# An mLSTM with two expert layers on one core: first gate chunk broadcast by masked matmuls, second gate round issued later, plain transposes, low bits on ScalarE

## The chip, the cores and the metric

One Trainium2 chip; the kernel runs on one core of it. The metric is the device time of one execution in microseconds (us): the median of three runs. Engines are named as in the profile: PE is TensorE (PEld its weight loads), DVE is VectorE, ACT is ScalarE, POOL is GpSimd, SP is SyncE, which issues every DMA of this kernel.

## What is computed

Three layers follow one another. The first is an mLSTM over 2 batches, 8 heads, 768 positions and head size 40, written in the reference as a recurrence:

```python
m_new = np.maximum(f_gate[:, :, t] + m, i_gate[:, :, t])
f_stab = np.exp(f_gate[:, :, t] + m - m_new)
i_stab = np.exp(i_gate[:, :, t] - m_new)
C = f_stab * C + i_stab * einsum('bhd,bhe->bhde', vt, kt)
n = f_stab * n + i_stab * kt
h_tilde = einsum('bhde,bhe->bhd', C, qt)
denom = np.maximum(np.abs(sum(n * qt)), 1.0)
y = sigmoid(o_gate) * h_tilde / denom
```

Its output, 1536 tokens of 320 features, goes through a layer of 2048 hidden units with a rational activation, P(h)/(Q(h) + 1e-6) with a cubic P and Q = 1 + |b0||h| + |b1|h^2 (weights w_in and w_out), and then through four ReLU experts of 1024 hidden units, whose outputs are summed with normalised probabilities.

## The kernel before

The mLSTM is worked in chunks of 128 positions: 6 chunks by 2 batches give 12 steps (`attn_steps`, i = 0 to 11, even i for batch 0). A step makes a decay matrix per head by a scan on DVE (`s_w`, L410) from forget gates that PE has broadcast over 128 partitions, multiplies it into q·k scores (`s_sc` L440, `s_pm` L445), multiplies by v scaled with the input gate (`s_v` L430, `s_pv` L470), adds the state carried from earlier chunks (`s_inter` L464), renews that state (`s_kend` L456 or L454, `s_delta` L485 to L490) and divides and gates the result (`s_y`, L498 to L505). `s_x` turns the 128 x 320 result into feature-major halves: `to_xT` transposes it on PE and splits it into a rounded part and a remainder (L526, L527). The features fill two blocks of 128 and one of 64. The last 64 are wanted twice, on both halves of the partitions: with DX=1 that is done by two full transposes (L521), one of 64 columns (L523) and one fp32 matmul into partitions 64 to 127 (L524, two passes in the trace).

The gates come in two rounds. `gates1` makes e = exp(...) for chunk 0 of all 16 rows (batch times head) in a tile of 48 partitions: forget gates in rows 0 to 15, input gates in rows 32 to 47. `gates1_bc(b)` broadcasts the forget gates of a batch's 8 heads with 8 fp32 matmuls (L302; 16 PE passes in the trace), and `gates1_ist` transposes the input gates. `gates2` does the other five chunks at once: a scan (L314), `gate_x` (five subtractions and additions on POOL, GX='G'), `exps` (two sigmoids on ACT, a reciprocal and a product on DVE), a scan (L321) and two calls of `expand`, which split the result into high and low parts and spread it with `mask` into the tiles fm and cm (L326 to L332). Step 2 is the first that reads fm (`bcast_f`, L344).

The first layer's weights come as 64-bit floats, seen as pairs of 32-bit integers. 22 pieces of 128 x 512 (`win_piece`, `wout_piece`) are loaded into two staging buffers (tag stg, SB=2) and converted by `conv64`: ACT takes the high word's magnitude (L187), POOL copies the high word (L199) and writes the top bits of the low word over it (L196; on ACT, L193, for one piece), DVE joins them (L201); then ACT rounds to fp32r (L159) and DVE or POOL subtracts for the remainder (L168). A staging buffer is free again after L187, L199 and L196 or L193 have read it.

The first layer runs in 48 units (`mono_unit`), each 16 matmuls of 128 x 256 (L544), an activation over ACT, DVE and POOL (`e_mono`) and 12 matmuls into an accumulator (L571 to L573). The experts follow: expert 0 in 24 units woven between the last mono units, then experts 1 to 3.

The order of the work is set by a table of times, KP. Every step, unit, piece and gate round is an event with a due time; events are emitted in that order (`emit`), which is the order of priority for the program's scheduler, and that fixes each engine's queue ahead of the run. GS, GD, SO, SO2, T1, PS, PP, MS, MP and TP are such times; letter strings such as L3, GLE, LO, SU, ve, ke, eh0 and el1 name the engine for each piece, unit or step. P0 is the number of pieces emitted ahead of everything but step 0's loads and gates.

Of the kernel before, what the change touches and what calls it, by code (L numbers as in the profile page):

```python
# [8 lines left out]
F32 = mybir.dt.float32  # L9
F32R = mybir.dt.float32r  # L10
AF = mybir.ActivationFunctionType
ALU = mybir.AluOpType
# [8 lines left out]
def kernel(  # L21
# [17 lines left out]
    P = 128  # L39
    B, NC, _, D = qk.shape[:4]  # L40
    H = kv.shape[4]
    S = NC * P
    DM = H * D
    NT = B * NC
    BH = B * H
# [9 lines left out]
    KP = dict(  # L55
        UP='PPPPPPPPPPPPPPPPPPPPPPPPPPPPPPPPPPPPPPPPPPPPPPPP',
        SU='GGGGGGGGGGGGGGGGGGGGGGGGGGGGGGVVVVVVVVGGGGGGGGGG',
        GLE='GGGGGGVGGGGGGGGGGGGGGGGGGGGGGGGGGGGGGGGVVGVGGGGG', L3='GGGGGGGGGGGGGGGGGGAGGG', P0=1, GS=2.5, GD=9.21,
        SO=1.69, SO2=13.47, T1=4.63, GX='G', KB=0, DA='VVVVVVVAAAAA', DX=1, ce='PPPPPPPPPPPP', CD=1, TG='SXX',
        TB=(2, 2, 2), HB=2, APR=0, APS=0, CPR=0, XPR=0, FPR=0, LPR=0, EPR=0, SG='GGGGGGGGGGGGGGGGGGGGGG',  # L60
        LO='VVGVVGVVGVVGVVGVVGVVGV', QC=1, qce='VGVVVVVVVVVV', cde='GGGGGGGGGGGG', ve='GGGGGGGGAGGG',
        ke='AGGGGGGGGGGA', xe='VVVVVVVVVVVV', XB=3, YB=4, RB=2, GB=2, FB=2, SB=2, VR=1, V1=2, XT=2, CB=2, LAGA=4,
        LAGB=4, TP=10.02, SP=1.13, MS=20.29, MP=5.0, PS=4.6, PP=1.11, LEAD=5, XR=0.69, XE=3, E0S=-6.11, E0P=2.33,
        E1S=1.27, eh0='AAGGAA', el0='VGVVVV', eh1='GAGGGG', el1='VGGGGG', qv=1.2, CVP='SSSSSSSSSSSSSSSSSSSSSS', EX='V', dv=-0.86, X2=1)
    YB, FB = KP["YB"], KP["FB"]

    V, A, G, PE, SY = nc.vector, nc.scalar, nc.gpsimd, nc.tensor, nc.sync

    ENG = dict(A=A, G=G, V=V)
# [37 lines left out]
    ident = cp.tile([P, P], F32, name="ident")  # L107
# [9 lines left out]
    sel = at1.tile([P, 2, 4], F32R, name="sel")  # L117
# [4 lines left out]
    mask = at1.tile([P, 4], F32, name="mask")  # L122
# [23 lines left out]
    def load_o(c):  # L146
        SY.dma_start(out=so[:, 2 * c:2 * c + 2, :], in_=o_gate[:, 2 * c:2 * c + 2, :])
# [17 lines left out]
    def split_lo(eng, dst, src, hi):  # L165
        k = n_conv[0] - 1
        eng = eng or (V if KP["CVP"][k] == "P" else ENG[KP["LO"][k]])
        eng.tensor_tensor(out=dst, in0=src, in1=hi.bitcast(F32), op=ALU.subtract)  # L168
# [91 lines left out]
    S0 = P + NA * P  # L260
    NX = NA * P
    n0 = 2 * S
    x1_, s11, s21, e1_ = [ga[0:48, n0 + n * P:n0 + (n + 1) * P] for n in range(4)]
    m_, gtmp = gb[0:BH, 0:S + 1], gb[0:BH, S + 1:2 * S + 1 - P]
    n0 = 2 * S + 4 - P
    d1, x2_, s12, s22 = [gb[0:112, n0 + n * NX:n0 + (n + 1) * NX] for n in range(4)]
    e2_, cd = [gc_[0:112, n * NX:(n + 1) * NX] for n in range(2)]
    fm, cm = [at1.tile([P, NA, 4, P], F32R, name=n) for n in ("fm", "cm")]
    ist = cp.tile([P, NC, BH], F32, name="ist")
    V.memset(m_[:, 0:1], -1e30)  # L270
    V.memset(x1_, 0.0)
# [10 lines left out]
    def gate_x(eng, a, z, outs):  # L282
        tmp = gtmp[:, 0:z - a]
        eng.tensor_tensor(out=tmp, in0=fr[:, a:z], in1=m_[:, a:z], op=ALU.add)
        for x, r, u, w in outs:
            eng.tensor_tensor(out=x[r:r + BH, 0:w - u], in0=tmp[:, u - a:w - a], in1=m_[:, u + 1:w + 1], op=ALU.subtract)
            eng.tensor_tensor(out=x[r + 32:r + 32 + BH, 0:w - u], in0=ir[:, u:w], in1=m_[:, u + 1:w + 1],
                              op=ALU.subtract)

    g1_last = []  # L290

    def gates1():
        V.tensor_tensor_scan(m_[:, 1:P + 1], fr[:, 0:P], ir[:, 0:P], -1e30, op0=ALU.add, op1=ALU.max)
        gate_x(V, 0, P, [(x1_, 0, 0, P)])
        exps(e1_, x1_, s11, s21)
        g1_last.append(V.memset(e1_[0:BH, 0:1], 0.0))

    def gates1_bc(b):
        bc = [(pa_p, f"acc{j}") if b == 0 else (ph_p, "h") for j in range(2)]
        bc = [p_.tile([P, U], F32, tag=t_, name=f"bc{b}") for p_, t_ in bc]  # L300
        for h in range(H):
            PE.matmul(bc[h // 4][:, (h % 4) * P:(h % 4 + 1) * P],  # L302
                      ident[0:BH, b * H + h:b * H + h + 1].to_broadcast([BH, P]), e1_[0:BH, :],
                      start=True, stop=True)
        bc_t[b] = bc

    def gates1_ist():
# [2 lines left out]
        V.tensor_copy(ist[:, 0, :], tp[:, 32:48])  # L310

    def gates2():
        with tc.issue_after(g1_last[0].ins):
            V.tensor_tensor_scan(m_[:, P + 1:S + 1], fr[:, P:S], ir[:, P:S], m_[:, P:P + 1], op0=ALU.add,  # L314
                                 op1=ALU.max)
        gate_x(ENG[KP["GX"]], P, S, [(x2_, 0, P, S0), (x2_, 64, S0, S)])
        exps(e2_, x2_, s12, s22)
        for r, a, z in ((0, P, S0), (64, S0, S)):
            V.tensor_copy(d1[r:r + BH, 0:z - a:P], e2_[r:r + BH, 0:z - a:P])
            V.memset(e2_[r:r + BH, 0:z - a:P], 0.0)  # L320
        V.tensor_tensor_scan(cd, e2_, d1, 0.0, op0=ALU.mult, op1=ALU.add)  # L321
        expand(cm, cd, s12.bitcast(F32R))
        expand(fm, e2_, s22.bitcast(F32R))
# [35 lines left out]
    def small_consts(last_sig):  # L359
        V.memset(cq, 1.0 + 1e-6)  # L360
        ab1 = cp.tile([P, 1], F32, name="ab1")
        rb1 = cp.tile([P, 1], F32, name="rb1")
        ab = cp.tile([P, 1], F32, name="ab")
        SY.dma_start(out=a_t, in_=dram_ap(moe_a, 0, [[0, P], [1, 4]]))
        SY.dma_start(out=b_t, in_=dram_ap(moe_b, 0, [[0, P], [1, 2]]))
        SY.dma_start(out=pr, in_=probs)
        A.activation(ab, b_t[:, 1:2], AF.Abs)
        V.tensor_scalar(ab1, ab, 1e-30, None, op0=ALU.max)
        with tc.issue_after(last_sig.ins):
            A.activation(rb1, ab1, AF.Abs_reciprocal_sqrt)  # L370
        V.tensor_tensor(out=sb1, in0=ab1, in1=rb1, op=ALU.mult)
        V.reciprocal(rb1, sb1)
        V.tensor_tensor(out=rb1, in0=rb1, in1=ab, op=ALU.mult)
        V.tensor_tensor(out=sb1, in0=sb1, in1=rb1, op=ALU.add)
        V.tensor_scalar(sb1, sb1, 0.5, None, op0=ALU.mult)
        psum_ = cp.tile([P, NT], F32, name="psum_")
        V.tensor_reduce(out=psum_, in_=pr, axis=AX.X, op=ALU.add)
        V.tensor_scalar(psum_, psum_, 1e-9, None, op0=ALU.add)
        V.reciprocal(psum_, psum_)
        V.tensor_tensor(out=pr, in0=pr, in1=psum_.unsqueeze(2).to_broadcast([P, NT, NE]), op=ALU.mult)  # L380
# [4 lines left out]
    def attn_steps(i):  # L385
        c, b = divmod(i, B)
# [3 lines left out]
        st = {}  # L390
# [51 lines left out]

        def s_pm(j):
            pm = st["W"][:, 4 * j:4 * j + 4, :]
            V.tensor_tensor(out=pm, in0=st["sc"][j], in1=pm, op=ALU.mult)  # L445

        def s_kend():
            if c < NC - 1:
# [47 lines left out]
        def s_y():  # L496
            o, den = st["o"], st["den"]
            V.reciprocal(den, den)  # L498
            so3 = so[:, i, :].rearrange("p (h d) -> p h d", h=H)
            if KP["xe"][i] == "V":  # L500
                G.tensor_tensor(out=so3, in0=so3, in1=den.to_broadcast([P, H, D]), op=ALU.mult)
            x = st["x"] = at2.tile([P, 384], F32, tag="x", bufs=KP["XT"], name=f"x{i}")
            x3 = x[:, 0:DM].rearrange("p (h d) -> p h d", h=H)
            if KP["xe"][i] == "V":
                V.tensor_tensor(out=x3, in0=o[:, :, 0:D], in1=so3, op=ALU.mult)  # L505
            else:
                for h in range(H):
                    A.activation(x3[:, h], o[:, h, 0:D], AF.Copy, scale=den[:, h])
                G.tensor_tensor(out=x3, in0=x3, in1=so3, op=ALU.mult)
            if not KP["DX"]:  # L510
                A.activation(x[:, DM:384], x[:, 2 * P:DM], AF.Copy)
# [68 lines left out]
    def e_mono(hp):  # L580
# [20 lines left out]
        A.activation(gh, s, AF.Copy)  # L601
        ENG[KP["GLE"][k]].tensor_tensor(out=gl, in0=s, in1=gh.bitcast(F32), op=ALU.subtract)  # L602
        return gh, gl
# [62 lines left out]
    ev = []  # L666
    steps = {i: attn_steps(i) for i in range(NT)}
    TP, SP = KP["TP"], KP["SP"]
    gates1()
    load_qkv(0)  # L670
    gates1_bc(0)
    gates1_ist()
    run(pieces, KP["P0"])
# [4 lines left out]
    ev.append((KP["GS"] + KP["GD"], gates2_ist))  # L678
    ev.append((KP["SO"], lambda: sig_o(0)))
    for c in range(1, NC):  # L680
        ev.append((KP["GS"] + 0.1, lambda c=c: load_o(c)))

    def sigs():
        for c in range(1, NC):
            ls = sig_o(c)
        small_consts(ls)
    ev.append((KP["SO2"], sigs))
    mu = [(g, j) for g in range(NG) for j in range(NUA)]
    t_end = [0.0] * NT
# [8 lines left out]
    t = KP["PS"]  # L698
# [3 lines left out]
    t = KP["MS"]  # L702
    na = 0
    while True:
        g, j = mu[na]
        t = max(t, t_end[2 * g + 1] + 0.2)
# [43 lines left out]
    x_acc = {}  # L750
    LAG[0] = KP["LAGB"]

# [16 lines left out]
    ev = []  # L769
# [3 lines left out]
    t = 0.0  # L773
# [24 lines left out]
    def e1_load():  # L798
        we[1] = expert_tile(1)
        for n, f in enumerate(expert_pieces(1, we[1], KP["eh1"], KP["el1"])):  # L800
            pri(KP["EPR"], f)
    ev.append((t_m + KP["E1S"], e1_load))
    emit(ev)
# [62 lines left out]
```

## Time and profile before

| | us |
|---|---|
| median of 3 runs | 694.28 (692.99 to 696.75) |
| the profiled execution | 695.96 |
| its span, first to last instruction | 693.9 |
| PE busy in the span | 645.6 (93%) |
| DVE busy | 376.5 (54%) |
| ACT busy | 309.3 (45%) |
| POOL busy | 262.8 (38%) |

The span and the busy times belong to the one profiled execution, 1.68 us above the median. A busy time is the sum over an engine's instructions; matmuls are pipelined, so the mean duration of one is longer than the distance from one to the next. Mean values over the whole span hide that the stages have different limits.

### The profile page before, as it was taken

What the parts mean: (1) busy time and instruction counts of PE and PEld (TensorE: products, weight loads), DVE (VectorE), ACT (ScalarE), POOL (GpSimd) and SP (SyncE); (2) the same over time, 40 slices, a digit from 0 to 9 for tenths busy, and PEclk for the clock granted to TensorE, in tenths of its full rate; (3) what the DMA queues carried; (4) which work ended last, traced back from release to release, by engine and by line L of the source; (5) the groups of instructions that cost most, each with busy time, mean ns of one, the idle gap of its engine ahead of it and who ended that gap; (6) DMA issues with size and microseconds to landing.
All of it is one profiled execution on the core that took longest, in us unless ns stands there. A gap on an engine that the chain in (4) does not pass through costs nothing.

```text
span 693.9 us, 10545 instructions
## 1 busy us (share of the span) xinstructions
PE 645.6 (93%) x4202; PEld 602.6 (87%) x4202; DVE 376.5 (54%) x602; ACT 309.3 (45%) x550; POOL 262.8 (38%) x255
## 2 busy tenths in 40 slices
PE   5467599999999799999999999999999999999997
PEld 5346489999999789999999999999999999999996
DVE  7887788786887877776576422222322222213132
ACT  5563666675667797676677422211111111111111
POOL 8687876454545653222223887730000000000000
PEclk9757699999999899999999999999999999999999
DMA  8756531111101400000000344300000000001011
GB/s 257 207 171 193 165 106 57 39 39 39 39 1 31 136 3 1 1 1 1 1 1 1 84 120 132 86 21 1 1 1 0 1 1 1 0 1 39 1 38 39
DMA packets 15697, 35.67 MB, mean 51 GB/s; under 512 B 2048, under 2 KB 7424, under 8 KB 15648
## 3 DMA queue, kind: packets, MB, share of 16 engines
q1 hardware_dynamic: 15648, 35.00, 17.0%
q8 instruction: 33, 0.54, 0.3%
q14 instruction: 16, 0.13, 0.1%
HBM read 33.03 MB, written 1.97 MB: 50 GB/s over the span
## 4 chain that ended last, share of the span: by engine, by line
PE 81%; DMA 6%; POOL 5%; DVE 4%; issue 1%; ACT 1%; SPq 1%; DVEq 0%; ACTq 0%; POOLq 0%
PE h L544 37%; PE acc L573 12%; PE acc L571 12%; PE acc L572 12%; DMA stg_a<-in_moe_w_in_dram 3%; PE o L470 2%; PE sc L440 2%; POOL cv_l L196 2%; DMA stg_b<-in_moe_w_out_dram 1%; POOL cv_l L199 1%; PE o L464 1%; PE tx L524 1%; DMA qkt<-in_qk_dram 1%; PE dl L485 1%; PE tx L521 1%
## 5 line engine op out<-in xcount | busy, mean ns | idle before, releaser
L544 PE MATMUL h<-x,we 128*128 128x512 f32 (+1 forms) x960 | 194.9, 349 | 0.0
L608 DVE SCALAR_TENSOR_TENSOR gl<-h,gh 128x512 fp32r<-128x512 f32 x96 | 66.3, 691 | 218.3 <-ACT gh L607 217.9
L544 PEld LDWEIGHTS h<-x,we 128*128 128x128 f32 x960 | 154.6, 189 | 19.2 <-issue 0.5
L607 ACT ACTIVATE gh<-h 128x512 fp32r<-128x512 f32 x96 | 57.3, 598 | 239.3 <-PE h L544 148.3
L572 PE MATMUL acc<-we,gh 128*128 128x320 f32 x384 | 117.0, 309 | 0.0
L571 PE MATMUL acc<-we,gh 128*128 128x320 f32 x384 | 116.8, 309 | 0.0
L544 PE MATMUL h<-x,win 128*128 128x256 f32 x768 | 106.0, 293 | 5.7 <-DVE s__2213 L598 4.7
L544 PEld LDWEIGHTS h<-x,win 128*128 128x128 f32 x768 | 100.5, 200 | 7.5 <-issue 5.3
L573 PE MATMUL acc<-we,gl 128*128 128x320 f32 x384 | 101.7, 310 | 0.0
L571 PEld LDWEIGHTS acc<-we,gh 128*128 128x128 f32 x384 | 72.2, 188 | 2.9 <-issue 0.3
L572 PEld LDWEIGHTS acc<-we,gh 128*128 128x128 f32 x384 | 72.2, 188 | 2.6
L573 PEld LDWEIGHTS acc<-we,gl 128*128 128x128 f32 x384 | 67.9, 188 | 0.1
L571 PE MATMUL acc<-wout,gh 128*128 128x320 f32 x192 | 60.5, 318 | 0.1
L572 PE MATMUL acc<-wout,gh 128*128 128x320 f32 x192 | 59.5, 312 | 0.0
L573 PE MATMUL acc<-wout,gl 128*128 128x320 f32 x192 | 56.4, 318 | 0.8 <-POOL gl L602 0.8
L440 PE MATMUL sc<-qkt 128*128 128x128 f32 x192 | 32.4, 328 | 6.1 <-DVE fb L410 5.5
L571 PEld LDWEIGHTS acc<-wout,gh 128*128 128x128 f32 x192 | 36.9, 192 | 0.7 <-ACT gh L601 0.4
L573 PEld LDWEIGHTS acc<-wout,gl 128*128 128x128 f32 x192 | 35.4, 190 | 2.1 <-POOL gl L602 1.6
L572 PEld LDWEIGHTS acc<-wout,gh 128*128 128x128 f32 x192 | 36.8, 192 | 0.3 <-issue 0.2
L440 PEld LDWEIGHTS sc<-qkt 128*128 128x128 f32 x192 | 29.9, 237 | 8.1 <-DVE fb L410 6.5
L201 DVE SCALAR_TENSOR_TENSOR cv_t<-cv_t,cv_l 128x512 int32<-128x512 int32 x22 | 18.8, 854 | 11.1 <-POOL cv_l L196 11.0
L410 DVE TENSOR_TENSOR_SCAN fb<-bf,id 128x512 f32<-128x512 f32 x20 | 23.7, 1209 | 1.0 <-PE bf L344 1.0
(759 smaller groups left out, 1012.9 us busy)
## 6 DMA issues: line engine op xcount, KB each, us to landing
stg_b<-in_moe_w_out_dram SPq DMA_DIRECT2D x10, 512.0 KB
stg_a<-in_moe_w_in_dram SPq DMA_DIRECT2D x8, 512.0 KB
stg_c<-in_moe_w_dram SPq DMA_DIRECT2D x8, 512.0 KB
kv<-in_kv_dram SPq DMA_DIRECT2D x12, 320.0 KB
qkt<-in_qk_dram SPq DMA_DIRECT2D x24, 160.0 KB
stg_d<-in_moe_w_dram SPq DMA_DIRECT2D x8, 480.0 KB
stg_a<-in_moe_w_in_dram SPq DMA_DIRECT2D x8, 256.0 KB
stg_c<-in_moe_w_dram SPq DMA_DIRECT2D x8, 256.0 KB
```

Of the source, the lines that this page charges most:

```text
L196: G.tensor_scalar(o, i_, 0.9375 / 32, 0.0, op0=ALU.mult, op1=ALU.add)
L199: G.tensor_scalar(l3.bitcast(F32), hw.bitcast(F32), 0.0, 1.0, op0=ALU.mult, op1=ALU.mult)
L201: V.scalar_tensor_tensor(out=ti, in0=ti, scalar=3, in1=l3, op0=ALU.logical_shift_left, op1=ALU.bitwise_or)
L410: V.tensor_tensor_scan(W, src, id4f, 0.0, op0=ALU.mult, op1=ALU.add)
L440: PE.matmul(sc[j][:, p, :], qkt[b][:, p, 2 * j], qT[:, p], start=True, stop=True)
L470: PE.matmul(o[:, h, :], st["W"][:, h, :], v1[:, h, :], start=(c == 0 and h == 0), stop=(h == H - 1))
L544: PE.matmul(o, w5[:, j, fs], r, start=(n == 0), stop=(n == len(seq) - 1))
L571: PE.matmul(acc[t], lh, wh, start=(first and a == 0), stop=False)
L572: PE.matmul(acc[t], lh, wl, start=False, stop=False)
L573: PE.matmul(acc[t], ll, wh, start=False, stop=(last and a == nff - 1))
L607: A.activation(gh, hp, AF.Relu)
L608: V.scalar_tensor_tensor(out=gl, in0=hp, scalar=0.0, in1=gh.bitcast(F32), op0=ALU.max, op1=ALU.subtract)
```

## The change

- The first gate round's broadcast: ACT and DVE split e into high and low parts (48 partitions), ACT spreads them with `mask` over four column blocks (tile fm1), and each half of a batch's heads is one fp32r matmul of 512 columns: four in all.
- The second gate round: its scan and `gate_x` are held until the second score product of step 0 (anchor p01), `gate_x` goes from POOL to DVE, and the rest is held until x of step 0 (anchor x0). Its due time goes from 2.5 to 10.3. The constants of the first layer are held until x of step 1.
- DX=0: before each transposition ACT copies the last 64 columns, and three plain transposes follow.
- L3: the low bits of all 22 pieces on ACT. P0=0: no piece ahead of step 1's loads. OL=8: gates o of chunks 1 to 5 are loaded later.
- Engines and times: GLE unit 6 to POOL and units 45 to 47 to DVE; remainder of piece 21 to POOL; pieces 7 to 10 keep their intermediate in PSUM, with the remainder on DVE; v of steps 0 and 1 scaled on ACT, of step 8 on POOL; expert 0's roundings all on ACT; one more of expert 1's remainders on DVE; T1, SO2, MP, XE, E1S and dv as below.

```diff
-        GLE='GGGGGGVGGGGGGGGGGGGGGGGGGGGGGGGGGGGGGGGVVGVGGGGG', L3='GGGGGGGGGGGGGGGGGGAGGG', P0=1, GS=2.5, GD=9.21,
-        SO=1.69, SO2=13.47, T1=4.63, GX='G', KB=0, DA='VVVVVVVAAAAA', DX=1, ce='PPPPPPPPPPPP', CD=1, TG='SXX',
+        GLE='GGGGGGGGGGGGGGGGGGGGGGGGGGGGGGGGGGGGGGGVVGVGGVVV', L3='AAAAAAAAAAAAAAAAAAAAAA', P0=0, GS=10.3, GD=9.21,
+        SO=1.69, SO2=16.65, T1=4.07, GX='V', KB=0, DA='VVVVVVVAAAAA', DX=0, ce='PPPPPPPPPPPP', CD=1, TG='SXX',
...
-        LO='VVGVVGVVGVVGVVGVVGVVGV', QC=1, qce='VGVVVVVVVVVV', cde='GGGGGGGGGGGG', ve='GGGGGGGGAGGG',
+        LO='VVGVVGVVGVVGVVGVVGVVGG', QC=1, qce='VVVVVVVVVVVV', cde='GGGGGGGGGGGG', ve='AAGGGGGGGGGG',
...
-        LAGB=4, TP=10.02, SP=1.13, MS=20.29, MP=5.0, PS=4.6, PP=1.11, LEAD=5, XR=0.69, XE=3, E0S=-6.11, E0P=2.33,
-        E1S=1.27, eh0='AAGGAA', el0='VGVVVV', eh1='GAGGGG', el1='VGGGGG', qv=1.2, CVP='SSSSSSSSSSSSSSSSSSSSSS', EX='V', dv=-0.86, X2=1)
+        LAGB=4, TP=10.02, SP=1.13, MS=20.29, MP=4.9, PS=4.6, PP=1.11, LEAD=5, XR=0.69, XE=2, E0S=-6.11, E0P=2.33,
+        E1S=2.92, eh0='AAAAAA', el0='VGVVVV', eh1='GAGGGG', el1='VVGGGG', qv=1.2, CVP='SSSSSSSPPPPSSSSSSSSSSS', EX='V', GA='x0', GB_='p01', SA='x1', OL=8, dv=-1.03, X2=1)
...
+    fm1 = cm[0:48, 0].rearrange("k n t -> k (n t)")
...
         g1_last.append(V.memset(e1_[0:BH, 0:1], 0.0))
+        hl = s11.bitcast(F32R)
+        A.activation(hl, e1_, AF.Copy)
+        V.tensor_tensor(out=hl[32:48], in0=e1_[0:BH], in1=hl[0:BH].bitcast(F32), op=ALU.subtract)
+        for n in range(4):
+            A.activation(fm1[:, n * P:(n + 1) * P], hl, AF.Copy, scale=mask[0:48, n:n + 1])
...
-        for h in range(H):
-            PE.matmul(bc[h // 4][:, (h % 4) * P:(h % 4 + 1) * P],
-                      ident[0:BH, b * H + h:b * H + h + 1].to_broadcast([BH, P]), e1_[0:BH, :],
-                      start=True, stop=True)
+        for hf in range(2):
+            q = 2 * b + hf
+            PE.matmul(bc[hf], sel[0:48, 0, q:q + 1].to_broadcast([48, P]), fm1, start=True, stop=True)
...
     def gates2():
-        with tc.issue_after(g1_last[0].ins):
+        with tc.issue_after(anchor[KP["GB_"]].ins):
             V.tensor_tensor_scan(m_[:, P + 1:S + 1], fr[:, P:S], ir[:, P:S], m_[:, P:P + 1], op0=ALU.add,
                                  op1=ALU.max)
-        gate_x(ENG[KP["GX"]], P, S, [(x2_, 0, P, S0), (x2_, 64, S0, S)])
+            gate_x(ENG[KP["GX"]], P, S, [(x2_, 0, P, S0), (x2_, 64, S0, S)])
+        with tc.issue_after(anchor[KP["GA"]].ins):
+            gates2_v()
...
-        ev.append((KP["GS"] + 0.1, lambda c=c: load_o(c)))
+        ev.append((KP["OL"], lambda c=c: load_o(c)))
...
-        small_consts(ls)
+        with tc.issue_after(anchor[KP["SA"]].ins):
+            small_consts(ls)
```

## Rows read from the trace of the kernel before

**Rows 1.** Busy time by stretch; the columns are named in the first line.

```profile
core 0: us, PE busy (x) PEld busy (x) DVE busy (x) ACT busy (x) POOL busy (x), PEclk, DMA share, GB/s
20.00:97.00 77.00, 47.00 (x267) 40.43 (x266) 61.53 (x102) 44.02 (x81) 63.32 (x72) 0.71 0.60 178
97.00:219.00 122.00, 121.36 (x925) 114.08 (x923) 99.42 (x171) 77.01 (x148) 64.21 (x73) 1.00 0.12 34
219.00:250.00 31.00, 26.32 (x180) 25.78 (x179) 25.66 (x36) 25.71 (x41) 19.61 (x15) 0.89 0.31 94
250.00:404.00 154.00, 153.03 (x1145) 149.46 (x1144) 100.40 (x152) 101.37 (x174) 60.03 (x45) 1.00 0.05 13
```

**Rows 2.** Chain of waits, 20 to 97: shares by line; pieces with start us, us.

```profile
by line: DMA stg_a<-in_moe_w_in_dram 28.9%; POOL cv_l L196 13.8%; DMA stg_b<-in_moe_w_out_dram 12.7%; POOL cv_l L199 11.0%; issue 7.6%; POOL kend L456 4.3%; POOL v L430 3.9%; DVE fb L410 3.1%; DVE cv_t L201 2.7%; POOL win L168 2.3%; POOL gl
...
11.19 9.39 DMA stg_a<-in_moe_w_in_dram
...
26.03 1.14 POOL cv_l L196
...
92.13 1.30 POOL cv_l L196
```

**Rows 3.** Waits in 20 to 97: waiter, released by, total, times, longest.

```profile
PE bf L344 <- ACT fm L332: 13.8, 1, 13.8
```

**Rows 4.** Transposition on PE inside the full stretch: start us, us, count last.

```profile
151.95 0.38 PE L521 MATMUL tx<-ident,x2n 128*128 128x128 f32 x2
152.17 0.27 PE L523 MATMUL tx<-ident,x2n 128*64 128x128 f32 x1
152.38 0.43 PE L524 MATMUL tx<-ident,x2n 128*64 128x128 f32 x2
152.74 0.45 PE L464 MATMUL o<-cst,qc 128*128 128x82 f32 x2
```

**Rows 5.** PE groups after 97: second passes of the transposition, count, then busy, mean ns.

```profile
L524 PE MATMUL tx<-ident,x2n 128*64 128x128 f32 x24 | 5.2, 298 | 0.0
...
L524 PE MATMUL tx<-ident,x 128*64 128x128 f32 x18 | 3.9, 298 | 0.0
```

**Rows 6.** Conversion groups in 20 to 97, by engine: busy, mean ns, idle before.

```profile
L196 POOL TENSOR_SCALAR cv_l<-stg_b 128x512 int16<-128x512 uint8 x10 | 9.5, 950 | 0.8
L196 POOL TENSOR_SCALAR cv_l<-stg_a 128x512 int16<-128x512 uint8 x10 | 9.4, 938 | 0.8
...
L199 POOL TENSOR_SCALAR cv_l<-stg_b 128x512 f32<-128x512 f32 x10 | 8.2, 820 | 5.8 <-DMA stg_b<-in_moe_w_out_dram 5.7
...
L187 ACT ACTIVATE cv_t<-stg_a 128x512 f32<-128x512 f32 x11 | 7.4, 672 | 10.5 <-DMA stg_a<-in_moe_w_in_dram 10.3 <-POOL wout L168 0.2
...
L193 ACT ACTIVATE cv_l<-stg_a 128x512 int16<-128x512 uint8 x1 | 0.8, 792 | 0.0
...
L201 DVE SCALAR_TENSOR_TENSOR cv_t<-cv_t,cv_l 128x512 int32<-128x512 int32 x21 | 17.8, 848 | 11.1 <-POOL cv_l L196 11.0
```

**Rows 7.** Opening stretch in order of time: start us, us, engine, line, count last.

```profile
2.10 0.43 SPq L216 DMA_DIRECT2D stg_a<-in_moe_w_in_dram  x1
...
4.60 0.31 ACT L277 ACTIVATE ga<-ga 48x128 f32<-48x128 f32 x1 [2.59 <-DVE ga L286]
...
7.66 3.75 PE L302 MATMUL bc<-ga,ident 16*128 16x128 f32 x16 [7.66 <-DVE ga L296]
...
9.74 1.22 DVE L410 TENSOR_TENSOR_SCAN fb<-bc,id 128x512 f32<-128x512 f32 x1 [0.59 <-PE bc L302]
...
38.70 1.22 PE L344 MATMUL bf<-fm,sel 112*128 112x512 f32 x2 [13.77 <-ACT fm L332]
```

**Rows 8.** DVE group in 20 to 97, 16 partitions of 384: busy, mean ns.

```profile
L328 DVE TENSOR_TENSOR gb<-gc,gb 16x384 fp32r<-16x384 f32 x4 | 3.0, 740 | 0.1
```

**Rows 9.** All instructions of L201 on DVE: min, median and max ns.

```profile
L201 DVE SCALAR_TENSOR_TENSOR cv_t<-cv_t,cv_l x22: 635/693/1641, 10.9 to 93.5; 128x512 int32<-128x512 int32 x22
```

More of the change, by code (lines that the diff above doesn't have):

```diff
@@ L290 @@
     g1_last = []
+    anchor = {}
     def gates1():
@@ L312, in gates2, with gates2_v @@
     def gates2():
-        with tc.issue_after(g1_last[0].ins):
+        with tc.issue_after(anchor[KP["GB_"]].ins):
             V.tensor_tensor_scan(m_[:, P + 1:S + 1], fr[:, P:S], ir[:, P:S], m_[:, P:P + 1], op0=ALU.add,
                                  op1=ALU.max)
-        gate_x(ENG[KP["GX"]], P, S, [(x2_, 0, P, S0), (x2_, 64, S0, S)])
+            gate_x(ENG[KP["GX"]], P, S, [(x2_, 0, P, S0), (x2_, 64, S0, S)])
+        with tc.issue_after(anchor[KP["GA"]].ins):
+            gates2_v()
+    def gates2_v():
         exps(e2_, x2_, s12, s22)
@@ L444, in s_pm @@
             pm = st["W"][:, 4 * j:4 * j + 4, :]
-            V.tensor_tensor(out=pm, in0=st["sc"][j], in1=pm, op=ALU.mult)
+            anchor["p%d%d" % (i, j)] = V.tensor_tensor(out=pm, in0=st["sc"][j], in1=pm, op=ALU.mult)
         def s_kend():
@@ L504, in s_y @@
             if KP["xe"][i] == "V":
-                V.tensor_tensor(out=x3, in0=o[:, :, 0:D], in1=so3, op=ALU.mult)
+                anchor["x%d" % i] = V.tensor_tensor(out=x3, in0=o[:, :, 0:D], in1=so3, op=ALU.mult)
             else:
```

## The prediction

> **What bounds the kernel now.** Read the busy times by stretch first [rows 1]. From 97 to 219 us and from 250 to 404 us PE is busy 121.36 of 122 us and 153.03 of 154 us at a granted clock of 1.00 (2.4 GHz): there the time is the sum of PE's own work, and ACT (77.01 and 101.37 us) and POOL have slack. From 20 to 97 us PE is busy only 47.0 of 77 us, at a mean granted clock of 0.71, while POOL is busy 63.32, DVE 61.53 and ACT 44.02. That is the conversion of the first layer's weights beside steps 2 to 5. A third, small stretch, 219 to 250 us, loses 4.7 us of PE, with DVE and ACT busy 25.7 of 31 each.
>
> Then the chain of waits through 20 to 97 us [rows 2]. It isn't PE's: it runs through the loads of staging buffers (28.9% + 12.7%, 32.0 of 77 us), and through POOL's L196 (13.8%, 10.6 us) and L199 (11.0%, 8.5 us), with more of POOL's in-order queue behind them (L456 and L430, 6.3 us). L196 stands in it 11 times, from 26.03 to 92.13 us. A staging buffer is reloaded only after POOL has read it twice, so POOL's queue sets the pace of the loads. The table of waits adds that PE stood 13.8 us, up to the start of step 2, for fm, the second gate round's result [rows 3].
>
> **The transposes.** In the full stretch one `to_xT` takes from 151.95 to 152.74 us, 0.79 us; its two L521 take from 151.95 to 152.17, 0.11 us each [rows 4]. Three plain ones are 0.33 us, so a block saves 0.46 us. L524 counts two passes a block, and 18 + 24 of them lie after 97 us [rows 5]: 21 blocks, 9.7 us, all where PE is the limit. The other three blocks lie where PE waits; costed at nothing. The price is an ACT copy of 128 x 64 a block. The nearest row is L277's 0.31 us for 128 columns [rows 7]; below, nothing. At 0.31 it is 24 x 0.31 = 7.4 us of ACT, hidden by the 45 and 53 us that ACT is idle in the two full stretches [rows 1]. If that cover is gone, the third transpose waits, and up to the whole 9.7 us comes back.
>
> **Low bits on ACT.** 21 of 22 pieces move; 20 of them in this stretch, 9.5 + 9.4 us of POOL, become 20 x 0.79 = 15.8 us of ACT [rows 6]. ACT comes to about 60 of 77 us, POOL to 44. On the chain 10.6 us of L196 go. What is late next is ACT's own reading of the buffer: L187 and L193 one after the other are 0.67 + 0.79 = 1.46 us, against 0.82 for L199 alone [rows 6], 0.64 more. If that comes last all 11 times it gives back 7.1 us; if POOL's L199 still comes last, nothing. So the gain is between 3.5 and 10.6 us; ACT is in order and waits for loads anyway, so I take the middle, 7.0.
>
> **Where the conversion begins.** With P0=0 the first load no longer leaves at 2.10 us [rows 7], ahead of step 0's q and k on SP's queue, but behind the loads of both first steps. Against that, OL=8 puts the o loads of five chunks behind the first pieces, and it is among these transfers that the next load took 9.39 us, to 20.6 us [rows 2]. So one conversion's lead is lost (up to 3.5 us: 77 us over 22 pieces) and the second load lands sooner (up to 2.5 us, if q and k and it shared that time); net zero, both ends kept.
>
> **The first gate round.** Its eight heads of a batch took 3.75 us [rows 7]. New: an ACT copy (0.31), a DVE subtraction (at most L328's 0.74 [rows 8]), four ACT copies (1.24), then matmuls of 512 columns, 1.22 us for two at 38.70 [rows 7]. The first scan, at 9.74 us before, 2.1 us after L302 began, could start 2.2 to 2.9 us after that point: the same or 0.8 us later. Batch 1 has no second 3.77 us ahead of it and gains up to 2.5 us. The load of 9.39 us spans that time, so I count nothing for it.
>
> **The second gate round.** `gate_x` becomes five DVE operations. L328, 16 x 384, takes 0.74 us [rows 8]; four of those and one of 640 are some 4.2 us on DVE, queued ahead of step 0's denominator and x, and of step 1's products. Behind x0, ACT's sigmoids wait, and conversions queue behind those. Before, the round's parts lay scattered among conversions until fm was ready at 38.6 us; later issue but undivided gives, by the same durations, 33 to 42 us. Step 2 may thus start 5 us sooner or 3 us later. But chain and wait overlap: POOL and the loads, not fm, carry the chain there [rows 2], so zero in the sum. Scaling v of steps 0 and 1 on ACT is 16 small operations, at most 16 x 0.31 = 5.0 us, in an ACT that in the opening waits for loads.
>
> **The rest.** Expert 0's two roundings on ACT are at most 4 x 0.67 = 2.7 us (L187's, 512 columns) where ACT is busy 25.71 of 31, and take a wait off POOL: -2 to +2, zero. GLE, LO, CVP, ve of step 8, MP, XE, E1S and el1 shift single operations into stretches where PE has over 99% [rows 1]: nothing. If E1S put expert 1's weights behind its first unit, PE would wait there; the two expert 0 units left over cover it.
>
> **The sum.** -9.7 - 7.0 = -16.7 us against the profiled 695.96 (span 693.9 and 2.06 around it): 679.3. The median of the runs is 1.68 lower, so the prediction is **677.6 us**. The unknowns give 669 to 687: the gain of the conversion at 10.6 and 2.5 us from the loads, to a gain of 3.5 less 3.5 for the later start, with 2 us from the experts' change either way.
>
> **The port.** L201 on DVE takes 0.635 us at best [rows 9] and 0.848 on average beside a busy POOL [rows 6]. The Trainium skill, SBUF — State Buffer, section "SBUF: two separate sides", says why: a DVE instruction with two SBUF inputs and a GpSimd one share a port pair, and the first to start holds it to its end. By that rule `gate_x` on DVE speaks against the change, since its five operations now shut POOL out, while L196 on ACT speaks for it; the trace shows only the slower L201, not the cause.
>
> **Rivals.**
> - *The conversion gets no shorter* (ACT's wait takes POOL's place, and the lead is lost): only the transposes count, 694.28 - 9.7 = 684.6. For: ACT already waits 10.3 us for one kind of load, so loads, not engines, may be the pace. Against: L196 is on the chain 11 times. Chance 0.20.
> - *DVE comes free as well*: without L196 beside it, 21 L201 save 0.848 - 0.635 each, 4.5 us, and no L196 is replaced (10.6): 694.28 - 9.7 - 15.1 = 669.5. For: DVE waited 11.0 us for L196 [rows 6]. Against: ACT must do two reads in its place. 0.13.
> - *The transposes give nothing*: the third waits for ACT's copy each time, so the change doesn't do there what it says: 694.28 - 7.0 = 687.3. Against: ACT idles over a third of those stretches. 0.07.
> - *Slower*: ACT's queue holds the staging buffers. L193 sits behind three reads of a unit's activation (3 x 0.67) at each of the 11 releases, so each costs 2.0 + 0.8 = 2.8 us: 30.8 less 10.6, +20.2, less 9.7, is +10.5: 704.8. It decides from (10.6 + 9.7 + 3.5)/11 = 2.2 us a release. Against: three units lie in that stretch, not eleven. 0.06.
> - The forecast: 0.54.
>
> The range 668 to 689 holds the forecast, the first three rivals and most of their unknowns. A measurement of this kernel can tell about 0.5% from no change: below 690.8 is faster, above 697.8 slower. Slower has 0.06; the same 0.06, taken from the worst ends of the first and third rival; faster 0.88.
>
> **What would show it.** The transposition's block from its first pass to the next line should take 0.33 us in place of 0.79, with no gap ahead of the third; the busy times should show PE's full stretch begin near 90 us in place of 97, with ACT near 60 and POOL near 44 of the same 77 us; the chain through 20 to 90 us should hold no L196 and more of ACT's L193 and of the loads. Wrong would be: the full stretch begins at 97 or later (first or last rival); PE waits for ACT ahead of the third transpose; or the wait of step 2 for fm ends well after 42 us.

## The result, and the profile after

The changed kernel takes 685.80 us (median of 4 runs, 685.00 to 687.47) against 695.51 us for the kernel before in the same batch (4 runs, 692.99 to 697.21): a ratio of 0.9866, with an interval of 0.9827 to 0.9906. Its profiled execution took 685.46 us with a span of 683.7 us, 10.2 us less than the span before. The forecast was 677.6 us, reckoned from 694.28 for the kernel before.

The busy times by stretch, against [rows 1]:

```profile
20.00:97.00 77.00, 52.67 (x283) 46.14 (x283) 66.03 (x115) 60.04 (x120) 44.40 (x53) 0.70 0.59 172
97.00:219.00 122.00, 120.87 (x935) 117.83 (x935) 100.94 (x172) 84.16 (x163) 69.18 (x74) 0.99 0.13 40
219.00:250.00 31.00, 24.50 (x170) 23.77 (x169) 25.89 (x37) 27.63 (x47) 17.99 (x14) 0.89 0.28 84
250.00:404.00 154.00, 152.32 (x1162) 151.94 (x1162) 100.87 (x151) 98.96 (x176) 57.34 (x43) 1.00 0.07 20
```

In the conversion's stretch ACT and POOL have changed places, to 60.04 and 44.40 us, as the prediction had it. DVE is at 66.03 of 77 us, 4.5 more than before. Finer windows of the same view show where PE's full stretch begins:

```profile
90.00:100.00 10.00, 8.11 (x44) 6.60 (x45) 9.94 (x17) 7.65 (x16) 7.20 (x9) 0.87 0.55 185
100.00:110.00 10.00, 9.48 (x71) 9.11 (x70) 7.97 (x13) 6.17 (x12) 6.61 (x8) 0.96 0.13 37
110.00:120.00 10.00, 10.00 (x83) 9.91 (x82) 9.23 (x17) 8.10 (x15) 7.01 (x8) 1.00 0.22 68
```

PE is full from some point between 100 and 110 us on, not from 90. From 100 to 110 us the kernel before had PE busy all 10.00 us. The granted clock, 0.87 and 0.96 in the first two of these windows, was 1.00 there before.

**Where the time went** is read best by following one piece of PE's work through both traces. The first-layer matmuls (L544 before, L554 after) of the same unit, counted from 0, start at these times; first the kernel before, then the one after, unit 6 in the timeline of PE:

```profile
118.68 0.40 PE L544 MATMUL h<-x,win 128*128 128x256 f32 x2
```
```profile
119.60 0.48 PE L554 MATMUL h<-x,win 128*128 128x256 f32 x2
```

Unit 6 starts 0.9 us *later* than before. Unit 19 starts 5.4 us sooner, unit 47 8.8 sooner, PE's last matmul 10.2 sooner. So the opening and the conversion together gave nothing, and 11.1 us came after 118 us, where PE is full.

The chain of waits through 20 to 97 us, against [rows 2], its shares by line:

```profile
by line: DMA stg_a<-in_moe_w_in_dram 28.3%; issue 8.6%; DMA stg_b<-in_moe_w_out_dram 6.9%; ACT cv_l L193 5.8%; POOL cv_l L199 5.6%; DVE win L168 3.7%; DVE cv_t L201 3.6%; DVE fb L455 3.3%; ACT cv_t L187 3.1%; DVE fb L420 2.9%; DVE gb L338 2
```

L196 is gone, L193 has come in, L187 has a larger share, and the loads' share fell from 41.6% to 35.2%. The groups of instructions of that stretch (busy, mean ns, idle before), against [rows 6]:

```profile
L193 ACT ACTIVATE cv_l<-stg_a 128x512 int16<-128x512 uint8 x10 | 7.8, 780 | 6.5 <-POOL cv_l L199 6.5
L193 ACT ACTIVATE cv_l<-stg_b 128x512 int16<-128x512 uint8 x10 | 7.7, 774 | 0.3 <-POOL cv_l L199 0.3
L199 POOL TENSOR_SCALAR cv_l<-stg_a 128x512 f32<-128x512 f32 x10 | 11.3, 1135 | 17.6 <-DMA stg_a<-in_moe_w_in_dram 17.6
L201 DVE SCALAR_TENSOR_TENSOR cv_t<-cv_t,cv_l 128x512 int32<-128x512 int32 x16 | 12.0, 762 | 5.5 <-ACT cv_t L187 3.7 <-ACT cv_l L193 1.8
```

POOL now waits 17.6 us for loads of stg_a alone, so over most of the stretch it isn't POOL that holds them up. But ACT's queue does in places. In the timeline of all engines:

```profile
28.68 0.65 POOL L199 TENSOR_SCALAR cv_l<-stg_b 128x512 f32<-128x512 f32 x1 [0.72 <-DMA stg_b<-in_moe_w_out_dram]
...
29.12 0.60 ACT L500 ACTIVATE cst<-dl 64x164 f32<-64x164 f32 x2
29.90 0.63 ACT L159 ACTIVATE win<-cv_t 128x512 fp32r<-128x512 f32 x1 [0.18 <-DVE cv_t L201]
30.51 0.63 ACT L159 ACTIVATE wout<-cv_t 128x512 fp32r<-128x512 f32 x1
31.04 0.64 ACT L187 ACTIVATE cv_t<-stg_b 128x512 f32<-128x512 f32 x1
...
31.59 0.77 ACT L193 ACTIVATE cv_l<-stg_b 128x512 int16<-128x512 uint8 x1
...
32.38 0.34 SPq L216 DMA_DIRECT2D stg_a<-in_moe_w_in_dram  x1
```

The piece had landed by 28.68 us. ACT, in order, first does step work and the copies of the pieces before it, and is done with the buffer at 32.36; only then does SP's queue issue the next load, at 32.38.

### The profile page after: what moved, and what is told of

The parts are those of the page before. It is cut to its first block, busy times and chain, and to the rows that moved or that the text cites. A ratio compares the mean times of both kernels' runs of the same rounds, so it can differ in the third digit from the quotient of the medians.

```text
span 683.7 us, 10419 instructions
## 1 busy us (share of the span) xinstructions
PE 630.8 (92%) x4126; PEld 595.2 (87%) x4126; DVE 375.9 (55%) x611; ACT 329.6 (48%) x610; POOL 229.4 (34%) x223
## 4 chain that ended last, share of the span: by engine, by line
PE 79%; DMA 6%; DVE 5%; ACT 5%; issue 2%; POOL 2%; SPq 1%; DVEq 0%; POOLq 0%; ACTq 0%
PE h L554 37%; PE acc L581 12%; PE acc L582 12%; PE acc L583 12%; DMA stg_a<-in_moe_w_in_dram 4%; PE o L480 2%; PE sc L450 2%; PE o L474 1%; DMA stg_b<-in_moe_w_out_dram 1%; ACT cv_l L193 1%; DVE fb L420 1%; PE dl L495 1%; POOL cv_l L199 1%; PE tx L531 1%; DMA stg_c<-in_moe_w_dram 1%
## 5 line engine op out<-in xcount | busy, mean ns | idle before, releaser
L554 PE MATMUL h<-x,we 128*128 128x512 f32 (+1 forms) x960 | 194.6, 348 | 0.0
L554 PEld LDWEIGHTS h<-x,we 128*128 128x128 f32 x960 | 154.4, 189 | 18.6
L554 PE MATMUL h<-x,win 128*128 128x256 f32 x768 | 106.5, 293 | 7.7 <-DVE s__2203 L608 5.5
L554 PEld LDWEIGHTS h<-x,win 128*128 128x128 f32 x768 | 100.7, 199 | 9.6 <-issue 5.8
L480 PE MATMUL o<-v,fb 128*128 128x41 f32 x192 | 27.5, 296 | 2.4 <-ACT cst L500 2.4
L480 PEld LDWEIGHTS o<-v,fb 128*128 128x128 f32 x192 | 26.9, 216 | 2.7 <-ACT cst L500 2.7
```

Of the source, the lines that this page charges most:

```text
L480: PE.matmul(o[:, h, :], st["W"][:, h, :], v1[:, h, :], start=(c == 0 and h == 0), stop=(h == H - 1))
L554: PE.matmul(o, w5[:, j, fs], r, start=(n == 0), stop=(n == len(seq) - 1))
```

## The experiments

A scheduler turns this program into the engines' queues, so a changed parameter also changes the order of everything else. Four kernels (e1 to e4) let it make the order anew. In those with "held" in the name, order-only edges (no wait for completion) keep each engine's queue in the order of the kernel named, and only the instructions that the edit replaces are placed freely. Each ratio is to the kernel before in the same batch (its medians there are 695.29 to 695.99 us), with its interval; differences to the kernel after (685.80) are between batches, and single executions of one kernel lie 2 to 6 us apart.

**The transposes alone, order made anew (e1).** Kernel before with `DX=1` made `DX=0`.

> The kernel before with DX=0 alone: an ACT copy of 128 x 64 and three plain transposes a block. Theory T (all of the change's gain is PE time saved by the transposes, some 0.46 us a block at full speed; the conversion got no shorter): 9 to 10 us below the kernel before, 684 to 687. Rival U (the conversion did get some 7 us shorter, and the later second gate round ate that): the same 9 to 10 us here, since neither is touched. Rival W (the transposes give back part in waits for the ACT copy): under 6 us, 690 or more.

Measured 698.24 us, ratio 1.0036 (1.0022 to 1.0050): slower, with less work for PE. PE was busy 118.04 us of 97 to 219 us, against 121.36 [rows 1], and unit 6 starts 5.3 us later than before. Part of the loss is a wait, with a fall of the granted clock behind it. From 140 to 150 us, first before, then in e1, with PE's wait:

```profile
140.00:150.00 10.00, 10.00 (x74) 9.28 (x74) 8.46 (x15) 7.97 (x20) 4.92 (x7) 1.00 0.01 2
```
```profile
140.00:150.00 10.00, 7.67 (x42) 7.08 (x41) 6.26 (x11) 3.34 (x6) 3.33 (x4) 0.73 0.10 31
142.81 0.49 PE L344 MATMUL bf<-fm,sel 112*128 112x512 f32 x1 [2.33 <-DVE fb L445]
```

PE stands 2.33 us. Then, though PE is busy throughout, the granted clock is 0.50 (1.2 GHz) from 145 to 151 us; over the whole window it is 0.73 where it was 1.00 (2.4 GHz), and PE has 42 matmul passes in it in place of 74. Between units 8 and 10 e1 falls 4.4 us further behind. As an experiment on the transposes it settles nothing, since the order moved with the edit.

**The old transposes in the kernel after, order made anew (e2).** `DX=0` made `DX=1`.

> The changed kernel with DX=1, the two transposes, the half transpose and the fp32 matmul of before. T: the gain is gone, 694 to 697. U: the same, 694 to 697. W: part of the gain stays, 688 to 692, since other edits of the change carry it.

Measured 699.49 us, 1.0072 (1.0047 to 1.0097): 13.7 above the kernel after, more than either theory has for that edit. Here too the order moved with the edit.

**Low bits back on POOL, order made anew (e3).** In the kernel after:

```diff
- L3='AAAAAAAAAAAAAAAAAAAAAA'
+ L3='GGGGGGGGGGGGGGGGGGAGGG'
```

> The changed kernel with the low bits back on POOL for 21 of 22 pieces. T (a staging buffer is held as long by ACT's queue as it was by POOL's): within 2 us of the changed kernel, 684 to 688. U (POOL's relief shortens the conversion by some 7 us): 691 to 694.

Measured 701.64 us, 1.0080 (1.0061 to 1.0098). One of its waits on PE shows that the loss isn't the conversion's alone; the waits from 97 to 420 us, first of the kernel after, then of this one:

```profile
PE h L554 <- DVE s__2203 L608: 5.5, 1, 5.5
```
```profile
PE h L554 <- DVE s__2203 L608: 10.5, 1, 10.5
PE bf L354 <- DVE fb L455: 5.0, 2, 4.3
```

At some 246 us, long after the conversion, PE stood 10.5 us for one operation of DVE's where it had stood 5.5.

**The second gate round early, order made anew (e4).** In the kernel after, `GS=10.3` made 2.5, `GX='V'` made 'G', and `gates2` issued behind the first round's last operation in place of `p01` and `x0`.

> The changed kernel with its second gate round as before: due time 2.5, no holding back behind steps 0 and 1, gate_x on POOL. T: step 2's scores start near 43 us in place of 51, but the time stays within 2 us of the changed kernel, 684 to 688, since the conversion, not step 2, sets when PE's full stretch begins. U: the 7 us that the hold ate come back, 677 to 680.

Measured 694.34 us, 0.9986 (0.9973 to 1.0000). Step 2's scores start at 41.0 us, 10.4 sooner than in the kernel after, and the kernel is still 8.5 slower. So an early step 2 alone doesn't make the kernel faster, though here too the order moved with the edit.

**The transposes alone, order held (e5).** As e1, in the order of the kernel before; the 24 ACT copies (12 of L511, 12 of L639) are free.

> The kernel before with DX=0 and every engine's queue held in the order of the kernel before; only the 24 ACT copies find their own places and the 24 extra matmuls are gone. Theory P (the block saves its 0.46 us wherever PE is full, and the first experiment's loss came from the order that the scheduler made anew): 8 to 10 us below the kernel before, 685.5 to 687.5. Rival Q (the third transpose waits for ACT's copy, or other waits fill the saved time whatever the order): 692 or more.

Measured 688.28 us, 0.9902 (0.9882 to 0.9922); the span is 685.6, 8.3 below before. In PE's timeline a block against [rows 4]:

```profile
150.13 0.49 PE L521 MATMUL tx<-ident,x2n 128*128 128x128 f32 x3
150.46 0.68 PE L464 MATMUL o<-cst,qc 128*128 128x82 f32 x5
```

It takes 0.33 us. Not every block does. This one waits for its copy, which stands behind L601 on ACT (timeline of PE and ACT):

```profile
212.43 0.64 ACT L601 ACTIVATE gh<-s__2076 128x512 fp32r<-128x512 f32 x1
212.50 0.38 PE L521 MATMUL tx<-ident,x 128*128 128x128 f32 x2
...
212.95 0.26 ACT L511 ACTIVATE x<-x 128x64 f32<-128x64 f32 x1
...
213.26 0.33 PE L521 MATMUL tx<-ident,x 128*128 128x128 f32 x1 [0.38 <-ACT x L511]
```

Unit 6 starts 1.1 us sooner, the end comes 8.3 sooner: 7.2 us after 118 us. Units 19 and 34 are 5.3 and 5.1 us sooner: between them nothing comes through, although four blocks lie there.

**The old transposes in the kernel after, order held (e6).** As e2; the ACT copies stay, so that only PE's part differs.

> The changed kernel with its queues' order held and its ACT copies kept, the last 64 columns transposed by the half transpose and the fp32 matmul of before. P: 9 to 10.5 us above the changed kernel, 695 to 696.5, the saved PE time and nothing else. Q: under 5 us above it, below 691. The second experiment, free to plan anew, gave 699.5.

Measured 693.53 us, 0.9988 (0.9971 to 1.0005): 7.7 above the kernel after, by median and by span. Unit 6 starts 1.0 sooner here than in the kernel after, so behind 118 us the plain transposes are worth 8.7. Its twelve runs fall in two groups, seven at 693.2 to 693.5 us and five at 696.2 to 696.5; the profile is of the first, and by the second the difference would be 10.5.

**Low bits back on POOL, order held (e7).** As e3.

> The changed kernel with 21 pieces' low bits on POOL again and the order of all other instructions held. P (POOL and ACT hold the staging buffers about as long; the third experiment's 701.6 came mostly from the new order): 685 to 691. Rival R (the move to ACT itself is worth what that experiment showed, since POOL's queue also carries the steps): 698 or more.

Measured 688.31 us, 0.9895 (0.9874 to 0.9917): 2.5 above the kernel after by median, 4.0 by span. Unit 3 starts 4.2 us later, unit 6 too, and every unit behind it 4.0 to 4.2:

```profile
123.77 0.48 PE L554 MATMUL h<-x,win 128*128 128x256 f32 x2
```

The span and the units are those of one execution each, this one 1.2 us above its median; the intervals of the ratios, 0.9874 to 0.9917 here and 0.9827 to 0.9906 for the kernel after, overlap. POOL's reads L199 of all pieces (min, median, max; first and last start), first before, then after, then this kernel:

```profile
L199 POOL TENSOR_SCALAR cv_l<-stg_a x12: 649/660/908, 6.4 to 81.8; 128x512 f32<-128x512 f32 x12
L199 POOL TENSOR_SCALAR cv_l<-stg_b x10: 643/692/1100, 25.3 to 89.3; 128x512 f32<-128x512 f32 x10
```
```profile
L199 POOL TENSOR_SCALAR cv_l<-stg_a x12: 636/668/2906, 12.8 to 85.7; 128x512 f32<-128x512 f32 x12
L199 POOL TENSOR_SCALAR cv_l<-stg_b x10: 649/908/1162, 24.7 to 92.6; 128x512 f32<-128x512 f32 x10
```
```profile
L199 POOL TENSOR_SCALAR cv_l<-stg_a x12: 648/795/3097, 13.2 to 89.4; 128x512 f32<-128x512 f32 x12
L199 POOL TENSOR_SCALAR cv_l<-stg_b x10: 641/713/1205, 25.8 to 96.9; 128x512 f32<-128x512 f32 x10
```

From first to last read the conversion takes 82.9 us before (89.3 - 6.4), 79.8 after (92.6 - 12.8) and 83.7 here (96.9 - 13.2). In the order of the kernel after, the low bits on ACT shorten it by 3.9 us. From the first read of a piece to the end of the last, its staging buffer is held 2.6 us on average before, 2.7 after and 2.9 here.

**Three buffers (e8).** Kernel after, order held, with `SB=2` made 3 and, for the room, `YB=4` made 3 and `XT=2` made 1.

> The changed kernel with its queues' order held and three staging buffers in place of two (YB=3 and XT=1 make the room). If two buffers set the pace of the conversion, whichever engine frees them: PE's full stretch begins some 5 us sooner and the time falls to 679 to 683. If ACT's and DVE's queues set the pace: within 2 us of the changed kernel, 684 to 688.

Measured 683.93 us, 0.9833 (0.9811 to 0.9854), the lowest median of all; its interval overlaps that of the kernel after. The third buffer hardly helps, and the timeline shows a reason:

```profile
44.13 0.64 POOL L199 TENSOR_SCALAR cv_l<-stg_b 128x512 f32<-128x512 f32 x1 [1.27 <-DMA stg_b<-in_moe_w_out_dram]
...
51.02 0.77 ACT L193 ACTIVATE cv_l<-stg_b 128x512 int16<-128x512 uint8 x1
```

A piece that had landed and been read by POOL at 44.13 us is read by ACT at 51.02. In this order, which was made for two buffers, a piece's place in ACT's queue holds it up, not the lack of a buffer. What three buffers would give in an order made for them isn't shown, nor what YB=3 and XT=1 cost.

**Transposes and low bits in the kernel before, order held (e9).** `DX=0` and all of L3 on ACT.

> The kernel before with its order held, DX=0, and all low bits on ACT: the two parts that the held runs priced, without any other edit of the change. Theory S (transposes 7.0 and low bits 2.5 us carry the whole change, the other edits come to nothing): 685 to 687 on the scale where the kernel before is 695.3. Rival M (in this order ACT's low bits save nothing or cost, since the order was made with them on POOL): 688 to 692; then the other edits are what makes room for them.

Measured 688.04 us, 0.9885 (0.9867 to 0.9903), against 688.28 for the transposes alone (e5), and a span of 686.5 against 685.6. In an order made with the low bits on POOL, moving them to ACT gives nothing: unit 6 starts 1.3 us later than in e5.

**The second gate round early, order held (e10).** As e4, with the round's 29 instructions alone free.

> The changed kernel with the order of everything else held, its second gate round (29 instructions) free, ahead of other work and with gate_x on POOL. S: within 2 us of the changed kernel, 684 to 688, though step 2's scores start some 5 us sooner. Rival U (the hold costs the conversion's gain): 679 to 682. Rival H (the hold helps, as the free run's 694.3 says): 690 or more.

Measured 686.16 us, 0.9856 (0.9840 to 0.9871): the same as the kernel after. Step 2's scores start at 50.0 us, 1.5 sooner; they wait for a scan on DVE (L420) in both, although the matmul that reads fm starts at 44.61 us here and at 49.33 in the kernel after. So holding the second round back costs nothing in this order.

**A due time moved by 0.01 (e11, e12).** `SP=1.13` made 1.14, nothing else, in the kernel after and in the one before, order made anew.

> The changed kernel, free, with the distance between a step's events at 1.14 in place of 1.13: the same instructions, a few in another order. If an order made anew is what moved the free runs by several us: 688 to 698. If such edits alone hardly move it: 684 to 688, and the losses of the free runs are the edits' own.

> The kernel before, free, with the same 1.14: 697 to 706 if the order made anew moves it, 694 to 697 if not.

Measured 685.37 us, 0.9846 (0.9829 to 0.9864), and 694.63, 0.9986 (0.9973 to 0.9998): 0.4 and 1.4 us from their kernels. But by tile and shape every queue of both holds its instructions in the old order, so in effect they are the same kernels again. They show how far the medians of the same work lie apart, and nothing on orders made anew; e1, by contrast, has some 570 of PE's 4154 matmul passes in other places. Between the same edit free and held lie 10.0 us (e1, e5), 6.0 (e2, e6), 13.3 (e3, e7) and 8.2 (e4, e10).

## Why the prediction was right, and where it wasn't

Faster it is, and 685.8 us lies in the range, but the forecast was 8 us too low, 1.2 of them because the kernel before took 695.51 in the result's batch. The change took 9.7 us off where 16.7 was forecast. What happened is nearest to the first rival, "the conversion gets no shorter", whose 684.6 is 1.2 off, by the sign that the prediction gave for it: PE's full stretch begins after 97 us. That it comes so near is partly luck: the transposes gave less than its 9.7, other edits made up for that, and the lead that it held lost was regained. The parts, by unit 6 as the divide:

- **Transposes, -9.7.** Right in place, a little small in yield: 7.2 us behind unit 6 in the order before (e5), 8.7 in the order after (e6). A block saves 0.46 us at 0.33, and more at 0.25 us; but blocks whose x or ACT copy is late give part of it back, as the prediction allowed, and in e5 the four blocks just ahead of and behind the stretch from 219 to 250 us, where PE isn't full [rows 1], yielded nothing. The ACT copy takes 0.26 us where 0.31 was the bound.
- **Low bits on ACT, -7.0.** The step that failed, together with the zeros for the rest of the opening and the conversion. It took POOL's 10.6 us off the chain and gave back only ACT's two reads. The runs show 4.2 us at unit 6 in the order of the kernel after (e7) and nothing in that of the kernel before (e9). And with the low bits back on POOL, unit 6 of e7 starts at 123.77 us, 5.1 later than before: the other edits, or the order that came with them, cost that much ahead of unit 6, where the sum had nothing, and the low bits on ACT give 4.2 of it back. Which of them costs it is open. What the step left out is that each of ACT's reads also stands behind ACT's other work: 3.7 us from landing to release at 28.68 us above, and on average a buffer is held no shorter than before (e7). The slower rival had that mechanism at 2.8 us for each of 11 releases; it is real, but not at every release.
- **Where the conversion begins, 0.** Right in the sum, though the first piece is read at 12.8 us in place of 6.4, later than the 3.5 us that it allowed. In SP's queue the first load now leaves at 6.03 us in place of 2.10 [rows 7], with a second load beside it:

```profile
6.03 0.96 SPq L216 DMA_DIRECT2D stg_a<-in_moe_w_in_dram  x2
...
12.76 0.65 POOL L199 TENSOR_SCALAR cv_l<-stg_a 128x512 f32<-128x512 f32 x1 [5.08 <-DMA stg_a<-in_moe_w_in_dram]
```

  From leaving to reading it takes 6.73 us (12.76 - 6.03), where it took 4.31 (6.41 - 2.10). But the second piece is read at 14.07 us, where it was read at 19.44 before. (The load that landed at 20.6 [rows 2] is the second half of the third piece, not the next load, as the prediction takes it.) By the eighth piece the late start is made up; POOL's read of it, first before, then after:

```profile
39.13 0.71 POOL L199 TENSOR_SCALAR cv_l<-stg_a 128x512 f32<-128x512 f32 x1 [0.24 <-DMA stg_a<-in_moe_w_in_dram]
```
```profile
39.12 1.09 POOL L199 TENSOR_SCALAR cv_l<-stg_a 128x512 f32<-128x512 f32 x1
```

  So the late start is not what took the gain of the low bits. The time is lost behind the eighth piece: the last is read at 92.6 us in place of 89.3.
- **First gate round, 0.** The four matmuls take 1.34 us where eight heads of one batch took 3.75 [rows 7]. But the first scan starts at 15.27 us in place of 9.74, because step 0's scores go first on PE and a conversion's L201 on DVE. What that costs was not tried alone.

```profile
11.71 1.34 PE L310 MATMUL bc<-cm,sel 48*128 48x512 f32 x4
```

- **Second gate round, 0.** Right in the sum, wrong in the time: step 2's wait for fm ends at 49.33 us, well after 42, which the prediction had named as a sign against it, and its scores start at 51.44. Yet holding the round back or not makes no difference in this order (e10). `gate_x` takes 3.9 us on DVE (1.09, 1.39 and 1.41 us), where 4.2 was estimated.
- **The rest, 0.** Behind unit 6 the kernel after gains 11.1 us, of which the transposes are 7.2 to 8.7. The other 2.4 to 3.9 us come from edits counted at nothing or from the new order; which of them is open. They set off part of what the conversion did not give.
- **"DVE comes free as well"** fell: L201 got faster (762 ns in place of 848, without the four pieces in PSUM), but `gate_x` and the steps fill DVE to 66.03 us, and some of POOL's L199 got much slower: 1135 ns on average for stg_a from 20 to 97 us, at a median of 668 over all twelve. The longest, 2906 ns from 36.24 us, ran beside L280, L201 and L168 on DVE, and ACT waited 2.27 us for it; that DVE slowed it isn't shown.

## What to carry to other kernels

When a scheduler remakes the order, price an edit with the queues held in a known order: here four edits came out 6 to 13 us slower with a remade order than with a held one, and a gain of 7 us was read as a loss. Moving a buffer's last reader from one in-order engine to another doesn't remove the wait; it swaps whose queue holds the buffer, so count what stands ahead of the read in the new queue, at every release. And a saving on the limiting engine counts only in the stretches where its busy time shows that it is the limit.

## What the runs showed that was not expected

Taking 24 matmuls off the engine that is full made the kernel 2.6 us slower (e1, 698.24 against 695.64 before) until the order was held (688.28). No single wait accounts for it: PE's unit 6 starts 5.3 us later, and behind it, up to 420 us, PE's five longest waits are 1.1 to 3.5 us; with the wait at 142.81 us went a fall of the granted clock (e1 above). Why the remade orders are worse as a whole stays open. And a third staging buffer, against a chain that is 35% loads, was worth only 1.9 us (e8), which lies within the noise.
